# A tenth weight tile in a stage buffer, the last tile contracted mode by mode, the first output pair moved in halves

## The chip, the cores and the metric

The kernel runs on one core of a Trainium2 chip. The time is that of the whole program on the device, in microseconds (us); the number that is compared is the median over several executions. A profile is one further execution, recorded by the hardware profiler. The engines are TensorE (PE; its weight loads are listed as PEld), VectorE (DVE), ScalarE (ACT), GpSimd (POOL) and SyncE (SP). Loads are issued from the queues of GpSimd and SP and are carried out by 16 DMA engines.

## The reference

Two steps follow each other. The first is causal attention with a decay:

```
scores = scale * q @ k^T + (cum[i] - cum[j])      # cum: running sum of log f, causal
x      = softmax(scores) @ v                      # (8 batches, 8 heads, 576, 64)
```

The heads are then laid side by side, so x is (8, 576, 512). The second step mixes in frequency:

```
X = rfft(x) along the 576 positions; the lowest 64 modes are kept
Y[b, m, :] = X[b, m, :] @ (w_r[m] + i w_i[m])     # 64 modes, each with two 512 x 512 matrices
y = irfft(Y)
u = x + y
out = u + relu(u @ w_ch)
```

The weights w_r and w_i are 64 x 512 x 512 float32 each, 134 MB together. The output is (8, 576, 512) float32, 9.4 MB.

## The kernel before, in words

**Weights.** The weights are cut into NT = 64 tiles of 1 MB in bf16 (2 MB as float32; the load casts). Tile n < 32 holds a quarter of the input channels for MG = 4 modes; a tile from 32 on holds half of the input channels for M2 = 2 modes. They go through a ring of NRING = 9 buffers (`wpool`, tag `wb`). `emit_w_load(n)` issues two loads per tile, one for w_r and one for w_i, both on GpSimd's queue in program order (`pool_dma`, L89). The last tile, 63, has four loads: each mode's w_r and w_i apart. A load waits until TensorE has read the tile that was in its buffer nine tiles before, and until the load eight places ahead of it on the queue has landed. `next_w` (L645) issues the next tile, and is called after each tile's contraction.

**Attention.** It runs over 32 steps `s`, each one head of two batches; two steps form a pair `pr` of heads. The k, q and v of a pair are loaded into one of STG = 3 stage buffers (`QKVst`, L202), pair `pr` into buffer `pr % 3`. Between the pieces of a step, from step 9 on, the kernel contracts weight tiles (`emit_modes`, L119): for each mode and each of four output blocks a few 16-column matmuls with the weights as the stationary operand, summed in a PSUM tile `A`, then added by VectorE to `Yacc` (tiles below 32) or to the transposed spectrum `YTe`/`YT2` (tiles from 32 on, L164).

**After attention.** The loop at L814 contracts tiles 32 to 62. Between the tiles it computes `XW` = x @ w_ch (`emit_xw`, L746), the rows y of the modes that are already complete (`emit_y`, `emit_mid`), and adds these modes' share of the inverse transform to x and XW (`emit_part`, L788). `emit_xw` keeps its transposed x in `yy`'s memory.

**The tail.** Only the last 16 modes (`YT2[:, 1]`) are then open. The output is made in 20 jobs (L926): for each pair of batches four jobs of 256 rows (two blocks in two PSUM banks) and one of 128 rows that holds the last 64 of both batches. A job sums u (= x + y) and z (= u @ w_ch) in two PSUM tiles of two banks each. Each row block has an x part (L884: an identity matmul of what is already known) and a y part (L885: the inverse basis times the last modes' rows). Then ScalarE copies u out (`emit_u`, L896), VectorE takes max(z, 0) + u (`emit_o`, L909), and SP stores the result (L919). `y_rows` (L718) makes the rows of four batches: four transposes into `ply` and four matmuls with w_ch into `plw`. Evacuating them needs the rows in other partitions than they come in: job 0's rows go straight to their slot in `yy` (L846, L847), the others into `yl` (L851, L852) and from there by small DMAs on GpSimd's queue (L855). `emit_late(0)` serves batches 0 to 3, `emit_late(1)` batches 4 to 7; the second follows job 0's turn of the loop at L944. That turn writes job 1's u, and turn n in general writes job n's z interleaved with job n+1's u. All PSUM tiles of the tail come from one pool of two buffers for each of the tags u and z (eight banks, L832); the tiles `A`, `ply` and `plw` take turns with the jobs' tiles in it.

Job 0's x part is also used to keep TensorE busy around the last tile: `fill(times)` (L932) repeats it, eight 64x64 matmuls of 512 columns each time, in two groups of four that run side by side. Before the change it is called four times before the last tile, once after it, and once after the row products.

Of the kernel before, what the change touches and what calls it, by code (L numbers as in the profile page):

```python
# [21 lines left out]
def kernel(  # L22
# [11 lines left out]
    nc = tc.nc  # L34
# [56 lines left out]

    def emit_w_load(n):
        dc, g = tile_of(n)
        if n < NTH:
            wb = wpool.tile([128, MG, 2 * D], BF16, tag="wb", name="wb")
# [7 lines left out]
        else:  # L103
            wb = wpool.tile([128, 2, M2, 2 * D], BF16, tag="wb", name="wb")
# [14 lines left out]
    def emit_modes(n):  # L119
# [3 lines left out]
        if late["psM"] is None:  # L123
            z = late["psZ"].tile([128, 2, D], F32, tag="u", name="A")
            A = z[:, 0, 0 : NDC * nm * 2 * B].rearrange(
                "p (e m c) -> p e m c", e=NDC, m=nm
            )
        else:
            A = late["psM"].tile([128, NDC, nm, 2 * B], F32, tag="A", name="A")
        if n < NTH:  # L130
            terms = [
                (lambda mi, es, r=r: wb[:, mi, r * D + es : r * D + es + 128],
                 lambda m, r=r: XT3s[dc][:, r, :, m])
                for r in (0, 1)
            ]
        else:
            terms = [
                (lambda mi, es, t=t, r=r: wb[:, t, mi, r * D + es : r * D + es + 128],
                 lambda m, c0=c0, r=r: XT3s[2 + r][:, m, c0 : c0 + 2 * B])
                for t, c0 in ((0, B), (1, 0))  # L140
                for r in (0, 1)
            ]
        for mi in range(nm):
# [15 lines left out]
        else:  # L159
            n8 = nm * 2  # L160
            w = HM if g >= GL else HM // 2
            yt = late["YTe"] if g >= GL else late["YTs"][2 * g // GL]
            c0 = g * n8 % w
            nc.vector.tensor_tensor(  # L164
                _strided(
                    yt[:, 0, 0, c0 : c0 + 1], [[B * w, NDC], [w, B], [1, n8]]
                ),
                _strided(A[:, 0, 0, 0:1], [[nm * 2 * B, NDC], [1, B], [B, n8]]),
                _strided(
                    Yacc[:, 0, g * nm, 0:1], [[NM * 2 * B, NDC], [1, B], [B, n8]]  # L170
                ),
                ALU.add,
            )

    with ExitStack() as actx:
# [26 lines left out]
        QKVst = [  # L202
            {
                nm: stq.tile(
                    [128, 2, NR, Dh], F32 if nm == "v" else BF16, name=f"st{nm}{i}"
                )
                for nm in "kqv"
            }
            for i in range(STG)
        ]  # L210
# [441 lines left out]
        for s in range(NS + 1):  # L652
# [5 lines left out]
            if s < 10 and nload < min(NRING, 3 + 3 * s // 4):  # L658
                next_w()
            if s == 9:  # L660
# [27 lines left out]
    with ExitStack() as bctx:  # L688
# [12 lines left out]
        yy = bsb.tile([128, 2, B // 2, 2, D], BF16, name="yy")  # L701
        yls = [bsb.tile([128, 2, D], BF16, name=f"yl{i}") for i in range(2)]

        def row_slot(q, j, t, i):
            p0 = HM * ((j + t) % 2) + H2 * i
            return yy[p0 : p0 + H2, 1, 2 * q + j // 2, t, :]

        yflat = yy[:, :, :, :, :].rearrange("p l b t e -> p (l b t e)")
        xTs = [
            yflat[:, i * NDC * SP : (i + 1) * NDC * SP].rearrange(  # L710
                "p (e s) -> p e s", e=NDC
            )
            for i in range(3)
        ]
# [23 lines left out]
        with ExitStack() as cctx:  # L738
# [75 lines left out]
            while nmode < NT - 1:  # L814
                emit_modes(nmode)
                nmode += 1
                next_w()
# [11 lines left out]
            for a, sb in parts[done:]:  # L829
                emit_part(a, sb)  # L830

        psZ = bctx.enter_context(  # L832
            tc.tile_pool(
                name="psZ", bufs=2, space=bass.MemoryType.PSUM, reuse_waits="tile"
            )
        )
        late["psM"], late["psZ"] = None, psZ


        def emit_late(q):  # L840
            ply = psZ.tile([128, 2, D], F32, tag="z", name="ply")
            plw = psZ.tile([128, 2, D], F32, tag="u", name="plw")[:, 0, :]
            ply = ply[:, 0, 0 : D // 2].bitcast(BF16)
            y_rows(YT2[:, 1], 4 * q, ply, plw)
            if q == 0:
                nc.vector.tensor_copy(row_slot(0, 0, 0, 1), ply[0:H2, :])  # L846
                nc.scalar.copy(row_slot(0, 0, 1, 1), plw[0:H2, :])  # L847
            return ply, plw

        def emit_moves(q, pl):  # L850
            nc.vector.tensor_copy(yls[q][:, 0, :], pl[0])  # L851
            (nc.scalar.copy if q else nc.vector.tensor_copy)(yls[q][:, 1, :], pl[1])  # L852
            for j in range(1 - q, 4):
                for t in range(2):
                    nc.gpsimd.dma_start(  # L855
                        row_slot(q, j, t, 1), yls[q][H2 * j : H2 * j + H2, t, :]
                    )

        def pieces(job):
            b, sb, nb, _ = job  # L860
# [11 lines left out]
        def start(job):  # L872
            return tuple(
                psZ.tile([128, 2, D], F32, tag=tag, name="p" + tag) for tag in "uz"
            )

        def terms(job, ps, t, what):
            b, _, nb, _ = job
# [17 lines left out]
        def emit_u(job, ps):  # L896
            uo = wpool.tile([128, 2, 2, D], F32, tag="wb", name="uo")
            nc.scalar.copy(uo[:, 0, 0 : job[2], :], ps[0][:, 0 : job[2], :])  # L898
            return uo

        def emit_o(job, ps, uo, last):
            b, sb, nb, ty = job
            pz = ps[1][:, 0:nb, :]
            u_sb, o_sb = uo[:, 0, 0:nb, :], uo[:, 1, 0:nb, :]
            if ty == "Q":
                nc.scalar.activation(o_sb, pz, ACT.Relu)
                nc.gpsimd.tensor_tensor(o_sb, o_sb, u_sb, ALU.add)
            else:
                nc.vector.scalar_tensor_tensor(  # L909
                    o_sb, pz, 0.0, u_sb, ALU.max, ALU.add  # L910
                )
            if sb == 4:
                for h in range(2):
                    eng = nc.scalar if last and h else nc.sync
                    eng.dma_start(
                        out[b + h, 512:576, :], uo[64 * h : 64 * h + 64, 1, 0, :]
                    )
            else:
                nc.sync.dma_start(  # L919
                    out[b, 128 * sb : 128 * sb + 256, :].rearrange(  # L920
                        "(p r) e -> p r e", r=2
                    ),
                    o_sb,
                )
# [5 lines left out]
        jobs = [(*j, ty) for j, ty in zip(jobs, "NNNNNNNNNNNNNNNNNNNN")]  # L930
        ps = start(jobs[0])
        def fill(times):  # L932
            for _ in range(times):
                run(terms(jobs[0], ps, 0, "x"), terms(jobs[0], ps, 1, "x"), pin=True)

        fill(4)
        emit_modes(nmode)
        fill(1)
        pl = emit_late(0)
        fill(1)  # L940
        run(terms(jobs[0], ps, 0, "y"), terms(jobs[0], ps, 1, "y"))
        uo = emit_u(jobs[0], ps)
        emit_moves(0, pl)
        for n, job in enumerate(jobs):  # L944
            last = n == len(jobs) - 1
            zs = terms(job, ps, 1, "xy") if n else []
            us = []
            if not last:
                nxt = start(jobs[n + 1])
                us = terms(jobs[n + 1], nxt, 0, "xy")  # L950
            if job[1] == 4:
                run(us)
                run(zs)
            else:
                run(zs, us)
            if not last:
                uo_n = emit_u(jobs[n + 1], nxt)
            emit_o(job, ps, uo, last)
            if not last:
                ps, uo = nxt, uo_n  # L960
            if n == 0:
                emit_moves(1, emit_late(1))
# [28 lines left out]
```

## Time and profile before

| | us |
|---|---|
| median of 4 runs (438.86 to 441.13) | 440.1 |
| the profiled execution | 440.77 |
| its span, first to last instruction | 438.7 |
| PE busy | 361.7 (82%) |
| PEld busy | 247.2 (56%) |
| DVE busy | 263.6 (60%) |
| ACT busy | 225.0 (51%) |
| POOL busy | 129.0 (29%) |
| last tile's contraction starts | 401.33 |
| first store issued | 407.45 |

Mean granted TensorE clock: 0.851. The DMA engines moved 97.33 MB by the queues' own count, which takes weights as bf16; HBM was read for 163.73 MB. Weights arrive by 65 loads of w_r and 65 of w_i (63 of 512 KB and two of 256 KB each), with a median of 16.4 and 17.9 us from issue to landing.

The page divides the span into 40 slices. A digit is the busy share of a slice in tenths; PEclk is the granted TensorE clock in the same way. In a timeline, a line has the start, the duration, the engine, the source line, the operation, what it writes and reads, and in brackets the idle time ahead of it with what ended it.

### The profile page before, as it was taken

How to read it: one execution, taken by the hardware profiler on the slowest of the kernel's cores; microseconds unless marked ns; L12 is line 12 of the kernel's file. 1: busy time of each engine (PE TensorE's matmuls, PEld its weight loads, DVE VectorE, ACT ScalarE, POOL GpSimd, SP SyncE). 2: the span in 40 equal slices, each digit the busy share in tenths (PEclk: the TensorE clock that was granted, in tenths of full speed). 3: DMA queues.
4: the chain of work that ended last, by engine and by line, in shares of the span. 5: the costliest groups of instructions: out<-in, count | busy, mean ns of one | idle time of the engine just before them, and what ended most of it. 6: DMA issues, size and time to landing. Idle time of an engine off the chain costs nothing.

```text
span 438.7 us, 12229 instructions
## 1 busy us (share of the span) xinstructions
PE 361.7 (82%) x5276; PEld 247.2 (56%) x5293; DVE 263.6 (60%) x656; ACT 225.0 (51%) x339; POOL 129.0 (29%) x202
## 2 busy tenths in 40 slices
PE   2687799999887976877878886999989788879984
PEld 1454666776665665655656665666655444444442
DVE  5687778878565665665557677333234444653684
ACT  3688368876544437436456373233425333632663
POOL 7333332153233223232332221432232222200500
PEclk9997589999877758758668598799999896998997
DMA  8999999999999999999999999999999999992797
GB/s 181 235 235 244 231 235 239 232 195 238 233 216 235 227 221 236 212 237 233 214 237 211 211 212 210 211 211 212 211 211 211 212 211 211 211 203 43 248 368 290
DMA packets 50037, 97.33 MB, mean 222 GB/s; under 512 B 3488, under 2 KB 12192, under 8 KB 49984
## 3 DMA queue, kind: packets, MB, share of 16 engines
q0 software_dynamic: 46688, 86.39, 100.6%
q1 hardware_dynamic: 3216, 10.04, 6.2%
q8 instruction: 41, 0.67, 0.6%
q10 hardware_dynamic: 80, 0.13, 0.1%
q14 instruction: 12, 0.10, 0.1%
HBM read 163.73 MB, written 9.44 MB: 395 GB/s over the span
## 4 chain that ended last, share of the span: by engine, by line
PE 33%; DMA 29%; DVE 10%; ACT 10%; issue 5%; POOL 1%; DVEq 0%; ACTq 0%
DMA wb<-in_moe_w_i_dram 26%; ACT E L517 7%; PE pav L555 7%; PE ps L510 6%; PE A L147 5%; PE tp L458 5%; DMA stv<-in_v_dram 3%; PE pz L734 2%; DVE QTs L473 2%; PE px L598 2%; DVE uo L909 2%; PE vp L482 2%; ACT KT L471 2%; PE pu L734 2%; DVE XT L612 1%
## 5 line engine op out<-in xcount | busy, mean ns | idle before, releaser
L517 ACT ACTIVATE E<-ps 128x1024 bf16<-128x1024 f32 (+1 forms) x128 | 101.6, 854 | 23.8 <-PE ps L510 14.2
L147 PE MATMUL A<-XT,wb 128*128 128x16 bf16 x2048 | 72.8, 181 | 15.7 <-DMA wb<-in_moe_w_i_dram 10.9
L147 PEld LDWEIGHTS <-wb 128*128 128x128 bf16 x2048 | 65.9, 100 | 30.6 <-issue 13.0
L90 POOL DMA_DIRECT2D wb<-in_moe_w_r_dram x65 | 43.3, 666 | 128.7 <-DMA wb<-in_moe_w_r_dram 22.0
L510 PE MATMUL ps<-QTs,KT 64*128 64x64 bf16 (+4 forms) x384 | 55.4, 313 | 18.3 <-ACT E L517 17.1
L90 POOL DMA_DIRECT2D wb<-in_moe_w_i_dram x65 | 43.2, 664 | 82.2 <-DMA wb<-in_moe_w_i_dram 43.2
L555 PE MATMUL pav<-va,E 128*128 128x65 bf16 (+1 forms) x1088 | 53.3, 206 | 4.0 <-DVE x_all L577 3.5
L555 PEld LDWEIGHTS <-E 128*128 128x128 bf16 (+1 forms) x1088 | 43.7, 111 | 19.8 <-issue 9.6
L532 DVE TENSOR_TENSOR E<-E,trimask 128x256 bf16<-128x256 bf16 (+2 forms) x128 | 37.2, 303 | 19.9 <-ACT E L517 19.6
L770 ACT CAST XW<-pxw 128x512 bf16<-128x512 f32 x36 | 20.7, 587 | 37.5 <-PE pxw L763 25.2
L475 ACT COPY VT<-tp 128x640 bf16<-128x640 bf16 (+1 forms) x32 | 23.1, 756 | 32.4 <-PE tp L458 32.3
L806 ACT CAST XW<-pB 128x512 bf16<-128x512 f32 x36 | 20.9, 586 | 32.2 <-PE pB L734 27.0
L510 PEld LDWEIGHTS <-KT 64*128 64x128 bf16 x384 | 18.9, 97 | 30.3 <-issue 21.0
L805 DVE CAST x_all<-pA 128x512 bf16<-128x512 f32 x36 | 24.9, 692 | 17.0 <-PE pA L734 15.1
L763 PE MATMUL pxw<-wch,yy 128*128 128x512 bf16 x133 | 33.9, 387 | 1.0 <-issue 0.3
L471 ACT COPY KT<-tp 128x640 bf16<-128x640 bf16 (+1 forms) x32 | 22.1, 752 | 22.3 <-PE tp L458 22.3
L473 DVE COPY QTs<-tp 128x640 bf16<-128x640 bf16 (+1 forms) x32 | 23.3, 768 | 14.2 <-PE tp L458 14.1
L577 DVE TENSOR_TENSOR x_all<-pav,rcp 128x384 bf16<-128x384 f32 x64 | 29.1, 454 | 0.8
L734 PEld LDWEIGHTS <-ident_bf 64*64 64x64 bf16 (+1 forms) x328 | 16.5, 111 | 19.2 <-issue 11.8
L909 DVE SCALAR_TENSOR_TENSOR uo<-pz,uo 128x1024 f32<-128x1024 f32 (+1 forms) x20 | 21.9, 1116 | 6.7 <-ACT uo L898 2.6
L164 DVE TENSOR_TENSOR YTe<-A,Yacc 128x128 bf16<-128x128 f32 x16 | 5.9, 367 | 32.5 <-PE A L147 32.5
L566 DVE RECIPROCAL rcp<-pav 128x6 f32<-128x6 f32 x64 | 12.1, 189 | 21.2 <-PE pav L555 20.4
(128 smaller groups left out, 639.6 us busy)
## 6 DMA issues: line engine op xcount, KB each, us to landing
wb<-in_moe_w_r_dram POOLq DMA_DIRECT2D x63, 512.0 KB, 16.4
wb<-in_moe_w_i_dram POOLq DMA_DIRECT2D x63, 512.0 KB, 17.9
stv<-in_v_dram POOLq DMA_DIRECT2D x15, 576.0 KB, 15.1
out_dram<-uo SPq DMA_DIRECT2D x16, 512.0 KB, 3.8
stk<-in_k_dram POOLq DMA_DIRECT2D x16, 288.0 KB, 15.1
stq<-in_q_dram POOLq DMA_DIRECT2D x16, 288.0 KB, 15.1
out_dram<-uo SPq DMA_DIRECT2D x7, 128.0 KB, 3.4
stv<-in_v_dram SPq DMA_DIRECT2D x1, 576.0 KB, 5.5
```

The source lines that it names most:

```text
L90: tc.keep_in_program_order(nc.gpsimd.dma_start(dst, src))
L147: nc.tensor.matmul(A[:, eb, mi, :], lhsT=w_of(mi, eb * 128), rhs=x_of(m), start=(i == 0), stop=(i == len(terms) - 1),)
L471: nc.scalar.copy(rows(KTs[pr % 2][:, :, 0:S]), tv)
L473: nc.vector.tensor_copy(rows(QT[pr][:, :, :]), tv)
L510: nc.tensor.matmul(ps[:, b, o : o + n], lhsT=KTs[pr % 2][bs, h, jb * 128 : (jb + 1) * 128], rhs=QT[pr][bs, h, jb * 128 + c0 : jb * 128 + c ...
L517: nc.scalar.activation(E[:, :, piece * 512 : piece * 512 + w], ps[:, :, 0:w], ACT.Exp, scale=scale,)
L532: nc.vector.tensor_tensor(dg, dg, tr, ALU.mult)
L555: nc.tensor.matmul(pav[64 * half : 64 * half + w, slot, :], lhsT=E[:, b, c : c + (w - 1) * st + 1 : st], rhs=va[:, jb, b, :], start=(n == ...
L577: nc.vector.tensor_tensor(xo, pi, ri, ALU.mult)
L734: return nc.tensor.matmul(p, lhsT=lhsT, rhs=rhs, start=first, stop=not first, skip_group_check=True)
L763: nc.tensor.matmul(pxw[:, :], lhsT=xT[:, eb, i * 128 : (i + 1) * 128], rhs=wch[:, eb, :], start=(eb == 0), stop=(eb == NDC - 1),)
L909: nc.vector.scalar_tensor_tensor(o_sb, pz, 0.0, u_sb, ALU.max, ALU.add)
```

## The change

Three things are changed, and with them the way PSUM is divided in the tail.

1. The second stage buffer (buffer 1 of 3) is taken from a tile `wx` of its own in a pool on the other side of SBUF. The last pair that it serves is pair 13, which is read in steps 24 and 25. At step 28 (`s == 2 * (NPR - 2)`) one weight tile more is loaded, into `wx`; it is tile 34. From then on each tile is issued one contraction earlier. After tile 34 itself no tile is issued. Once tile 35 has been contracted, `open_late` closes `wx` and opens `yy` and `yls`, which were opened at the start of the phase before.
2. Tile 63 is contracted mode by mode and, within a mode, w_r before w_i, so that each group of eight matmuls needs one of the four loads. VectorE adds each mode by itself (`add_y`). The fillings are spread: one before the tile, one after mode 0, two between the w_r and w_i of mode 1, and half a one (u alone) after it: 36 matmuls instead of 48. The first matmul of mode 1 waits for VectorE's addition of mode 0.
3. Job 0's u is copied in two halves, and its result taken and stored in two halves. `ply` and `plw` have PSUM tiles of their own (`psL`), and job 1's u tile (`psU`) is free from the start; its z tile (`psX`) takes `psL`'s banks once `ply` and `plw` are read. ScalarE copies `ply` and VectorE does the two copies of `plw`. Job 1's u is written ahead of job 0's z rows, and job 1's z ahead of job 2's u. The rows of batches 4 to 7 are made after the sums of turn 3, in the second banks of job 4's two tiles, which that job does not use; they are copied by ScalarE after turn 3 and by VectorE after job 4's result, and their eight moves are issued then.

```diff
+    def wb_tile(n, *dims):
+        if n != late.get("nx"):
+            return wpool.tile([128, *dims], BF16, tag="wb", name="wb")
...
+        return late["wx"][:, 0 : math.prod(dims)].rearrange(
...
+        if n == NT - 1:
+            for mi in range(nm):
+                m = g * nm + mi
+                for hf, half in enumerate((terms[:2], terms[2:])):
+                    for w_of, x_of in half:
+                        for eb in range(NDC):
+                            tc.keep_in_program_order(
+                                nc.tensor.matmul(
+                                    A[:, eb, mi, :],
+                                    lhsT=w_of(mi, eb * 128),
+                                    rhs=x_of(m),
+                                    start=(eb == 0 and w_of is terms[0][0]),
...
+                    fill(mi, hf)
+                add_y(mi, mi + 1)
+            return
...
+            if s == 2 * (NPR - 2):
+                late["nx"] = nload
+                next_w()
...
                 emit_modes(nmode)
+                if nmode != late["nx"]:
+                    next_w()
                 nmode += 1
-                next_w()
+                if nmode == NTH + GL // 4:
+                    open_late()
...
-        def emit_u(job, ps):
+        def emit_u(job, ps, split=False):
             uo = wpool.tile([128, 2, 2, D], F32, tag="wb", name="uo")
-            nc.scalar.copy(uo[:, 0, 0 : job[2], :], ps[0][:, 0 : job[2], :])
+            for i in range(2 if split else 1):
+                bs = slice(i, i + 1) if split else slice(0, job[2])
+                nc.scalar.copy(uo[:, 0, bs, :], ps[0][:, bs, :])
...
-        fill(4)
-        emit_modes(nmode)
-        fill(1)
-        pl = emit_late(0)
-        fill(1)
-        run(terms(jobs[0], ps, 0, "y"), terms(jobs[0], ps, 1, "y"))
-        uo = emit_u(jobs[0], ps)
-        emit_moves(0, pl)
+        def fill(mi, hf):
+            for _ in range((1, 0, 1, 2, 0)[2 * mi + hf + 1]):
+                run(*(terms(jobs[0], ps, t, "x") for t in range(2)), pin=True)
+            if mi + hf == 2:
+                run(terms(jobs[0], ps, 0, "x"), pin=True)
+
+        fill(0, -1)
+        emit_modes(nmode, fill)
+        ply = psL.tile([128, D], BF16, tag="A", name="ply")
+        plw = psL.tile([128, D], F32, tag="plw", name="plw")
+        y_rows(YT2[:, 1], 0, ply[:, :], plw[:, :])
+        nc.vector.tensor_copy(row_slot(0, 0, 0, 1), ply[0:H2, :])
+        nc.scalar.copy(yls[0][:, 0, :], ply[:, :])
+        emit_moves(0, 0, (1,))
+        run(terms(jobs[0], ps, 0, "y"))
+        nc.vector.tensor_copy(row_slot(0, 0, 1, 1), plw[0:H2, :])
+        nc.vector.tensor_copy(yls[0][:, 1, :], plw[:, :])
+        emit_moves(1, 0, (1,))
...
+        lctx.close()
+        psPair[1]["z"] = psum(bctx, "psX")
+        uo = emit_u(jobs[0], ps, True)
         for n, job in enumerate(jobs):
...
-            if job[1] == 4:
+            if n == 0:
+                run(us)
+                run(zs)
+            elif n == 1:
+                run(zs)
+                run(us)
+            elif job[1] == 4:
                 run(us)
                 run(zs)
             else:
                 run(zs, us)
+            if n == 3:
+                y_rows(
+                    YT2[:, 1], 4, nxt[1][:, 1, 0 : D // 2].bitcast(BF16), nxt[0][:, 1, :]
+                )
             if not last:
                 uo_n = emit_u(jobs[n + 1], nxt)
-            emit_o(job, ps, uo, last)
+            emit_o(job, ps, uo, n == 0, last)
+            if n == 3:
+                nc.scalar.copy(yls[1][:, 1, :], nxt[0][:, 1, :])
+            if n == 4:
+                nc.vector.tensor_copy(
+                    yls[1][:, 0, :], ps[1][:, 1, 0 : D // 2].bitcast(BF16)
+                )
...
-            if n == 0:
-                emit_moves(1, emit_late(1))
```

## The prediction

> **What bounds the kernel now.** I read the time slices of the page first, then busy time by stretch, the GpSimd queue's own timeline, and last VectorE's timeline and the chain of waits at the end. The slices:
>
> ```profile
> DMA  8999999999999999999999999999999999992797
> GB/s 181 235 235 244 231 235 239 232 195 238 233 216 235 227 221 236 212 237 233 214 237 211 211 212 210 211 211 212 211 211 211 212 211 211 211 203 43 248 368 290
> ```
>
> The 16 DMA engines are busy without a gap for 35 of 40 slices, at a flat 211 GB/s once only weights move. Those are bytes as bf16; the fp32 side is twice that, 422 GB/s. So the program is 400 us of loads and then a tail of 38 us, in which slice 37 (395 to 406 us) moves almost nothing. By stretch (the last three numbers are the granted clock, the DMA share and GB/s):
>
> ```profile
> 265.00:275.00 10.00, 6.29 (x142) 5.29 (x139) 7.24 (x19) 1.85 (x4) 1.82 (x3) 0.76 1.12 211
> ...
> 393.00:396.00 3.00, 1.76 (x42) 1.13 (x38) 1.12 (x2) 1.12 (x2) 0.00 (x0) 1.00 0.77 144
> 396.00:400.00 4.00, 4.00 (x31) 1.54 (x32) 1.75 (x3) 1.17 (x2) 0.00 (x0) 0.57 0.43 79
> 400.00:401.00 1.00, 1.00 (x24) 0.50 (x20) 0.00 (x0) 0.00 (x0) 0.00 (x0) 1.00 0.06 16
> ```
>
> The engines do not finish together: the share sinks from 393 on and the last bytes come at 400. The last four loads, issued at 378.22, 380.43, 382.98 and 385.45, take 18.1, 17.1, 15.9 and 14.7 us, so they land at 396.3, 397.5, 398.9 and 400.15. TensorE is then at half clock. GpSimd's queue at the end of attention, where the new buffer acts:
>
> ```profile
> 259.97 0.72 POOL L90 DMA_DIRECT2D wb<-in_moe_w_i_dram  x1
> 265.93 0.71 POOL L90 DMA_DIRECT2D wb<-in_moe_w_r_dram  x1 [5.24 <-PE A L147]
> 266.64 0.72 POOL L90 DMA_DIRECT2D wb<-in_moe_w_i_dram  x1
> 274.62 0.71 POOL L90 DMA_DIRECT2D wb<-in_moe_w_r_dram  x1 [7.25 <-PE A L147]
> ```
>
> GpSimd waits 5.24 and 7.25 us for TensorE to free a ring slot. Yet the DMA share in that stretch is 1.12, the same as everywhere. VectorE in the tail:
>
> ```profile
> 404.68 0.69 DVE L852 CAST yl<-plw 128x512 bf16<-128x512 f32 x1 [0.60 <-ACT yy L847]
> 406.20 1.23 DVE L909 SCALAR_TENSOR_TENSOR uo<-pz,uo 128x1024 f32<-128x1024 f32 x1 [0.83 <-ACT uo L898]
> 407.34 0.42 DVE L851 COPY yl<-ply 128x512 bf16<-128x512 bf16 x1
> 409.39 2.43 DVE L909 SCALAR_TENSOR_TENSOR uo<-pz,uo 128x1024 f32<-128x1024 f32 x2 [1.64 <-issue]
> 412.22 1.82 DVE L909 SCALAR_TENSOR_TENSOR uo<-pz,uo 128x1024 f32<-128x1024 f32 x2 [0.40 <-PE pz L734]
> 414.64 1.22 DVE L909 SCALAR_TENSOR_TENSOR uo<-pz,uo 128x1024 f32<-128x1024 f32 x1 [0.60 <-ACT uo L898]
> ```
>
> From 416.16 on the same pattern returns every 6.76 us (416.16, 422.92, 429.68). The chain there alternates TensorE's z sums with VectorE's results and has no spare engine in it, so a shift of job 6's result reaches the end whole.
>
> **What the Trainium skill says.** "DMA: Bandwidth & Descriptors", Specifications, gives 435 GB/s as the fabric's ceiling for a core. The trace agrees: 422 is 97% of it, so earlier issue cannot raise the rate. The same page, "Why a DMA increments its semaphore by 16 and not by 1": a load counts as landed only when all 16 engines have posted. The share sinking for 7 us ahead of the landing at 400.15 fits. "TensorE: Matmul & The Clock Gate", Part 1: the clock is halved or restored by activity over a free-running window of about 3.4 us. The trace has half clock from about 396.4 to 399.9. "PSUM — Partial Sum Buffer", Terms: two engines may not be on one bank and quadrant at once. This fits the wait that the change adds between the two modes, which share a bank; the trace before has no such wait.
>
> **The extra weight tile: nothing.** Tile 34 goes to the stage buffer at step 28 without waiting for a slot, so each later tile is issued one slot earlier, and the waits of 5.24 and 7.25 us should shrink or go. The bytes and the 130 weight loads are the same, in the same queue order. When GpSimd issued again at 274.62, how far was the DMA from idling? At 279.88 it waits for the landing of the load of 259.97; loads take about 2.45 us each (0.5 MB at 211 GB/s), so those of 265.93 and 266.64 land near 282.3 and 284.8. There were 10 us in hand. The cover is this backlog; without it, the loss would be at most the excess of a wait over it. Value taken 0; between 0 and -1 if in other executions the quick DMA engines run dry. The new waits of GpSimd on VectorE (stage buffer read by step 25) are past by then. The pool opened late (yy, yls) waits only for tile 34's matmuls, six tiles ahead of its first use.
>
> **The last tile, mode by mode: +0.25.** Before, TensorE ran 32 filling matmuls (8 steps of four, 0.42 us a step at half clock and 0.21 at full) from 399.09 to 401.22, and only then the tile from 401.33 to 402.28. So TensorE, not the landing at 400.15, was late. Afterwards the same 32 filling matmuls stand in between: 0.85 at half clock to 399.94, mode 0 (16 matmuls of 0.03, and 0.1 for the switch, 401.22 to 401.33 above) to 400.53, two steps to 400.96, 8 matmuls to 401.30, four steps to 402.16, the last 8 to 402.50. Then VectorE adds half a tile: 0.37 less 64 x 1.06 ns (0.681 against 1.224 us for 512 and 1024 elements) is 0.30, from 402.55 to 402.85. Filling of two steps runs beside it to 402.93, and the transposes follow 0.1 later, near 403.0 against 402.77. The new wait (mode 1 behind VectorE's add of mode 0) holds all of TensorE's queue, but two filling steps and the switch, 0.53, cover its 0.35. Without that cover it would cost about 0.3. With all waits on DMA instead of filling, the gain would be 24 matmuls, 0.7; with the clock still low, the loss 0.5. I keep -0.7 to +0.5.
>
> **First job and the rows.** Call the first transpose P (402.77 before). Before, in us after P: job 0's result 3.43 to 4.66, job 1 at 6.62, job 2 at 7.85, job 3 at 9.45, job 5 at 11.87, job 6's z sum starts at 11.59 and its result at 13.39. Job 1's u had waited for the evacuation of the second u bank (start 405.42, just after the cast of 404.68 ended), and its z stood behind the second row product (8 matmuls from 406.40 to 407.5) and interleaved with job 2's u.
> Afterwards: rows ready at 0.44 (transposes) and 1.29 (product). VectorE copies 0.44 to 0.85, casts twice 0.69 (a cast's time goes by free size) to 2.67; ScalarE copies to about 1.1 (128x512, 0.59 to 0.74). TensorE, no longer waiting for a bank: job 0's u rows to 1.53, job 1's u (4 steps) to 2.4, job 0's z rows to 2.83, job 1's z to 3.7, job 2's u to 4.56. ScalarE: two halves of 0.586 to 2.74 (0.16 more than one of 1.014), then job 1 to 3.75. VectorE: halves of 0.62 (0.681 and 1.224 bound them) from 2.86 to 4.1, job 1 to 5.33. Job 2 waits for ScalarE (4.76 to 5.77): result 5.8 to 7.03. Job 3's z stands beside job 4's u, whose bank ScalarE frees at 5.77: result near 7.4. So job 1 leads by 2.5, jobs 2 and 3 by 2.05.
> GpSimd's moves: the one for jobs 2 and 3's u is issued at 1.15 and lands 1.7 later, needed at 3.95; the one for their z at 2.77, landing at 4.5, needed at 4.8. Four more follow at 0.5 each, needed from 8.5. SP has one more store to issue, 24 instead of 23; stores land in 2.7 to 4.5 us and nobody waits for their slots within nine jobs.
>
> **The second rows: the lead mostly goes back.** Before, the product for the second half of the batches sat in VectorE's bubble of 1.64. Now it comes after job 3's sums. TensorE: from 7.13, 1.2 for the product to 8.35 (406.40 to 407.60), job 5's u to 9.2, job 4's z to 9.65; so job 4's result ends at 10.5 and the cast of its bank's other half, 0.42, at 10.95. Only then is the bank free, and job 6's z starts at 11.0, against 11.59: 0.59 earlier. The eight moves for this half are issued from 11.05 instead of 5.3, and job 10 needs the first at 15.6. They took 1.7 to 4.9 us before, so at worst 0.4 late.
>
> **The sum.** 0 + 0.25 - 0.59 = -0.35. The profiled execution took 440.77 (span 438.7 and 2.07 around it), so 440.4; that execution is 0.67 above the median, so against 440.1 it is 439.7. With the bounds of its terms and the spread of the runs (438.86 to 441.13), 438.9 to 440.6.
>
> **Rivals.** (1) The lead of 2.05 survives, because the product of the second rows finds TensorE idle. For it: TensorE idles 0.3 to 0.5 at several places in each period. Against: 1.2 + 0.42 stand in one chain in front of job 6's bank. 438.05 on the median. (2) The extra tile does work: the landing comes up to 2 us sooner because the quick engines no longer run dry and less is left to the slow ones. For it the two waits, against it the share of 1.12. About 438. (3) Slower: the clock. Twelve filling matmuls fewer (36 instead of 48) and more waits among the first jobs; if one more window of 3.4 us falls to half clock there, 1.75 us of TensorE work is lost. It decides from a fifth of a window on (0.35 of 1.75). One window gives 441.5, two 443.2. Against it: 1.00 was granted from 400 to 434 although TensorE was busy 85% of 409 to 434. (4) The change does not do what it says: the tile in the stage buffer lands no sooner. That is part of the forecast.
>
> **How the numbers follow.** Forecast 0.53, rival 1 0.25, rival 2 0.08, rival 3 0.14. The range 438.0 to 441.3 holds almost all of the first, about half of rivals 1 and 2 and a third of rival 3, some 0.8. A change of 0.5%, 2.2 us, is about what a measurement of this kernel can tell from none: bounds 437.9 and 442.3. Below the lower one falls half of rival 1, half of rival 2 and 0.03 of the forecast, 0.20; above the upper one about 0.6 of rival 3 and 0.01 of the forecast, 0.10; between them 0.70.
>
> **What would show it.** Right: GpSimd's waits on TensorE between 255 and 278 gone and DMA share still 1.12; last landing near 400; transposes at about 403.0; job 1's result some 4.2 after them; job 4's result late by TensorE and job 6's z started by the cast of its bank. Wrong: a landing before 399, a half clock in the tail, a wait for moved rows at job 10, or job 4 following job 3 without a gap.

## The result, and the profile after

The changed kernel takes 442.68 us (median of 38 runs, 439.64 to 445.7) against 439.4 us for the kernel before (59 runs, 437.88 to 443.13). The ratio is 1.0065, with a 95% interval of 1.005 to 1.008: by this ratio 2.9 us slower, where 439.7 (438.0 to 441.3) was predicted. The runs of the changed kernel also lie further apart, over 6.1 us instead of 5.3, and 16 of the 38 are above 443. The profiled execution took 441.33 (span 439.3). It is one of the quicker ones, and the one of before was one of the slower, so the two spans differ by only 0.6. Three executions of the experiments below lay far above the others of their kernel (663.18 of again, the one that was profiled, 556.48 of filled_wait and 445.05 of product_later); they are in the medians of the table, but not in its ratios nor in the counts of executions.

The slices of the changed kernel, DMA share and GB/s:

```profile
DMA  8999999999999999999999999999999999991798
GB/s 180 235 235 243 232 236 238 235 218 230 236 212 237 233 215 237 208 237 236 211 237 211 211 211 211 211 211 211 212 211 210 212 211 211 211 191 36 242 363 295
```

The load phase is as it was: 211 GB/s without a gap. GpSimd's queue at the end of attention:

```profile
267.27 0.71 POOL L90 DMA_DIRECT2D wb<-in_moe_w_r_dram  x1 [2.59 <-PE A L185]
...
276.32 0.71 POOL L90 DMA_DIRECT2D wb<-in_moe_w_r_dram  x1 [6.49 <-PE A L185]
...
283.65 0.72 POOL L90 DMA_DIRECT2D wb<-in_moe_w_r_dram  x1 [3.87 <-PE A L185]
```

The waits on TensorE did not go. Before, the three long ones were 3.51, 5.24 and 7.25 us (at 259, 266 and 275); now they are 2.59, 6.49 and 3.87, each some 9 us later, 13.0 in all instead of 16.0. The last four loads are issued at 377.40 to 385.58 (before: 378.22 to 385.45). So nothing was lost there and little could be won. Now VectorE's timeline in the tail of the changed kernel (start, duration, instruction, and in brackets the idle time ahead of it):

```profile
402.96 0.41 DVE L989 COPY yy<-ply 32x512 bf16<-32x512 bf16 x1 [0.65 <-PE ply L772]
...
405.36 2.42 DVE L953 SCALAR_TENSOR_TENSOR uo<-pz,uo 128x512 f32<-128x512 f32 x3
409.80 2.50 DVE L953 SCALAR_TENSOR_TENSOR uo<-pz,uo 128x1024 f32<-128x1024 f32 x2 [2.02 <-issue]
413.83 0.69 DVE L953 SCALAR_TENSOR_TENSOR uo<-pz,uo 128x512 f32<-128x512 f32 x1 [1.53 <-PE pz L785]
414.44 0.41 DVE L1030 COPY yl<-pz 128x512 bf16<-128x512 bf16 x1
414.84 1.22 DVE L953 SCALAR_TENSOR_TENSOR uo<-pz,uo 128x1024 f32<-128x1024 f32 x1
416.70 2.43 DVE L953 SCALAR_TENSOR_TENSOR uo<-pz,uo 128x1024 f32<-128x1024 f32 x2 [0.63 <-PE pz L785]
```

P, the first transpose of the last rows, is 402.53 here and was 402.77. Job 0's two halves and job 1 follow from 405.36, that is P + 2.83, as predicted (2.86). Then comes a gap of 2.02 that was not predicted: job 2's result starts at P + 7.27 instead of P + 5.8. From there the lead is gone, and job 6's result starts at P + 14.17, where it was P + 13.39 before. What holds job 2 stands in TensorE's timeline:

```profile
407.04 0.38 PE L785 MATMUL pu<-XW,ident_bf 64*64 64x512 bf16 x1
408.87 0.40 PE L785 MATMUL pz<-yy,BIl 64*64 64x512 bf16 x2 [1.45 <-DMA yy<-yl]
...
411.08 0.38 PE L772 MATMUL pz<-ident_bf,YT 128*128 128x128 bf16 x4
...
414.91 0.40 PE L785 MATMUL pz<-x_all,ident_bf 64*64 64x512 bf16 x1 [0.31 <-DVE yl L1030]
```

TensorE stands still for 1.45 us until a move of rows (`yy<-yl`) has landed. The second product (411.08) overwrites a half of job 2's z banks, so it waits for job 2's result (409.80 to 411.03). Behind the product come the sums of job 4, its result (413.83) and the cast that VectorE makes next (414.44); job 6's z sums (414.91) wait for that cast. The whole wait is handed down to the end.

Why is that move late? The queues at that time, GpSimd's and ScalarE's, and the stores on SP's:

```profile
404.60 2.98 POOL L900 DMA_DIRECT2D yy<-yl  x6 [18.49 <-ACT yl L990]
413.72 3.91 POOL L900 DMA_DIRECT2D yy<-yl  x8 [6.14 <-ACT yl L1028]
```

```profile
403.41 0.59 ACT L990 COPY yl<-ply 128x512 bf16<-128x512 bf16 x1 [4.67 <-DVE yy L989]
```

```profile
406.08 2.06 SPq L965 DMA_DIRECT2D out_dram<-uo  x3
```

In the source the move that job 2's z needs (product rows of batch 1) is the second of the six. In the built program it is the fourth. This is GpSimd's instruction order with the semaphores (counters) that each waits for, and the matmul of job 2's z that waits for the move. Activation and DVE are the counters of ScalarE and VectorE; a DMASW counter is raised when a move lands:

```
191 L900 DMACopy yy<-yl_5118 32x512 [waits DMASW2_49,Activation_49,Pool_49]
192 L900 DMACopy yy<-yl_5118 32x512 [waits DMASW3_49]
193 L900 DMACopy yy<-yl_5118 32x512 [waits DMASW4_49]
194 L900 DMACopy yy<-yl_5118 32x512 [waits DMASW5_49,DVE_49]
...
10029 L785 Matmult pz<-yy,BIl 64x512 [waits DMASW5_49]
```

The first three are the transposed rows (they need ScalarE's copy only); the product rows, which need VectorE's cast, come after them. The six are issued 0.5 us apart, the fourth at 406.11. From issue to landing the six took 1.7, 1.7, 1.7, 2.7, 3.1 and 2.8 us: the fourth is the first that meets job 0's stores, issued from 406.08 on. 406.1 plus 2.7 is the 408.8 at which TensorE goes on. (ScalarE's copy, 403.41, also began 0.44 later than predicted: it waited for VectorE's copy out of the same `ply`.)

The program of the kernel before has the same order of the six, with this move fourth. There it was issued at P + 3.50, no store was issued before 407.45 (P + 4.68), the move landed after 1.7 us, and job 2's z sums read the rows only at about P + 6.0. The change asks for them at P + 4.9 and, by halving job 0's result, sends the first store off at P + 3.55.

### The profile page after: what moved, and what is told of

Its sections match the earlier page's. It is cut to its first block, busy times and chain, and to the rows that moved or that the text cites. A ratio compares the mean times of both kernels' runs of the same rounds, so it can differ in the third digit from the quotient of the medians.

```text
span 439.3 us, 12210 instructions
## 1 busy us (share of the span) xinstructions
PE 359.4 (82%) x5263; PEld 246.4 (56%) x5281; DVE 263.9 (60%) x658; ACT 225.2 (51%) x340; POOL 128.9 (29%) x202
## 4 chain that ended last, share of the span: by engine, by line
PE 31%; DMA 30%; ACT 12%; DVE 10%; issue 5%; POOL 1%; DVEq 0%; ACTq 0%
DMA wb<-in_moe_w_i_dram 26%; ACT E L558 8%; PE pav L596 6%; PE ps L551 5%; PE A L185 5%; PE tp L499 5%; DMA stv<-in_v_dram 3%; PE px L639 2%; DVE QTs L514 2%; ACT KT L512 2%; PE pz L785 2%; PE vp L523 2%; DVE uo L953 1%; DVE XT L653 1%; PE pu L785 1%
## 5 line engine op out<-in xcount | busy, mean ns | idle before, releaser
L185 PE MATMUL A<-XT,wb 128*128 128x16 bf16 x1984 | 70.4, 181 | 15.9 <-DMA wb<-in_moe_w_i_dram 11.1
L185 PEld LDWEIGHTS <-wb 128*128 128x128 bf16 x1984 | 63.5, 99 | 30.2 <-DMA wb<-in_moe_w_i_dram 12.2
L90 POOL DMA_DIRECT2D wb<-in_moe_w_r_dram x64 | 42.4, 663 | 126.7 <-PE A L185 24.2
L90 POOL DMA_DIRECT2D wb<-in_moe_w_i_dram x64 | 42.2, 660 | 81.2 <-DMA wb<-in_moe_w_i_dram 40.4
```

The costliest lines, as they stand in the source:

```text
L90: tc.keep_in_program_order(nc.gpsimd.dma_start(dst, src))
L185: nc.tensor.matmul(A[:, eb, mi, :], lhsT=w_of(mi, eb * 128), rhs=x_of(m), start=(i == 0), stop=(i == len(terms) - 1),)
```

## The experiments

The kernels ran in three groups (four rows of the table each), every group beside its own runs of the kernel before, whose median was 439.65, 439.55 and 439.51. P is read from each kernel's own profile.

| kernel | median | ratio to before (95%) |
|---|---|---|
| again | 442.29 | 1.0066 (1.0039 to 1.0092) |
| moves_in_order | 439.49 | 0.9999 (0.9979 to 1.0018) |
| no_extra_tile | 442.6 | 1.0063 (1.0034 to 1.0092) |
| extra_tile_alone | 438.82 | 0.9989 (0.9972 to 1.0007) |
| changed_again | 441.9 | 1.006 (1.004 to 1.0079) |
| filled_wait | 441.61 | 1.0042 (1.0023 to 1.0061) |
| moved_third | 440.4 | 1.0016 (0.9997 to 1.0035) |
| product_later | 439.49 | 0.9999 (0.9983 to 1.0015) |
| first_moves_in_order | 439.55 | 1.0 (0.9986 to 1.0014) |
| second_moves_in_order | 442.96 | 1.0093 (1.0062 to 1.0124) |
| filled_four | 441.55 | 1.0047 (1.0029 to 1.0066) |
| fewer_fillers | 438.08 | 0.9981 (0.9966 to 0.9996) |

### Late moves, or the load phase?

**again** is the changed kernel, without an edit.

> The changed kernel once more, for a second profile of it beside the ones below. Theory M (late moves): the move of the product's rows for batch 1 stands fourth in GpSimd's queue, so TensorE's z sums of job 2 wait over 1 us for it (1.45 us in the first profile), and job 6 comes late with it. Theory L (load phase): the extra tile lets the last weights land later in some executions (400.5 to 403 instead of 399.9). Both expect 442.7 median; M expects the wait in this profile again, 1 to 4 us, and the last contraction at the same 398.8 to 399.5; L expects the last landing to have moved, and the tail behind it not.

It gave times only. 442.29 repeats the result.

**moves_in_order** pins each move behind what is already on GpSimd's queue:

```diff
     def emit_moves(t, q, js):
         for j in js:
-            nc.gpsimd.dma_start(
+            tc.keep_in_program_order(nc.gpsimd.dma_start(
                 row_slot(q, j, t, 1), yls[q][H2 * j : H2 * j + H2, t, :]
-            )
+            ))
```

> The changed kernel with the 14 moves of rows issued in the order of the source, so that the product's rows for batch 1 go second and not fourth. M: the move is issued at P + 2.7 instead of P + 3.6 (P is the first transpose of the last rows), its rows land 1.0 to 1.5 us sooner, job 2's z sums no longer wait, and the whole is 1 to 1.5 us faster than the changed kernel: about 441.3. L: nothing changes, 442.7.

439.49: the whole loss is gone, twice what the wait of 1.45 explains. The order on the other engines is the same to the instruction. VectorE's and GpSimd's timelines of this kernel, where P is 402.80:

```profile
408.55 2.58 DVE L953 SCALAR_TENSOR_TENSOR uo<-pz,uo 128x1024 f32<-128x1024 f32 x2 [0.50 <-ACT uo L946]
412.58 0.69 DVE L953 SCALAR_TENSOR_TENSOR uo<-pz,uo 128x512 f32<-128x512 f32 x1 [1.45 <-PE pz L785]
413.19 0.41 DVE L1030 COPY yl<-pz 128x512 bf16<-128x512 bf16 x1
413.62 1.23 DVE L953 SCALAR_TENSOR_TENSOR uo<-pz,uo 128x1024 f32<-128x1024 f32 x1
415.46 2.43 DVE L953 SCALAR_TENSOR_TENSOR uo<-pz,uo 128x1024 f32<-128x1024 f32 x2 [0.62 <-PE pz L785]
```

```profile
404.87 0.52 POOL L900 DMA_DIRECT2D yy<-yl  x1 [19.71 <-ACT yl L990]
405.80 2.45 POOL L900 DMA_DIRECT2D yy<-yl  x5 [0.41 <-DVE yl L994]
```

The move is issued at 405.80 and lands 1.7 us later, at 407.5; TensorE's first matmul that needs it runs at 407.51. Job 2's result is at P + 5.75 and job 6's at P + 12.66, 1.5 us sooner after P than in the changed kernel's profile and 0.7 sooner than before. That the median is still only as good as before has to do with what lies ahead of P (see the last tile, below).

**no_extra_tile** leaves the tail as changed and takes the extra load of part 1 out; all weight tiles come from the ring of nine again, and `yy` and `yls` are opened at the start of the phase (the second stage buffer stays in its own pool):

```diff
-        if n != late.get("nx"):
+        if True:
             return wpool.tile([128, *dims], BF16, tag="wb", name="wb")
...
-            if s == 2 * (NPR - 2):
-                late["nx"] = nload
-                next_w()
...
+        wxctx.close()
+        open_late()
...
-                if nmode != late["nx"]:
-                    next_w()
+                next_w()
                 nmode += 1
-                if nmode == NTH + GL // 4:
-                    open_late()
```

> The changed kernel without its first part: no weight tile in the stage buffer, everything after the loads as in the changed kernel. M: as the changed kernel, 442.7 within 0.7. L: as before or below it, 439 to 440.5.

442.6: the loss stays, so it is not the extra tile's.

**extra_tile_alone** is the kernel before with part 1 alone (`wb_tile`, `stage`, `open_late` and the load at step 28):

> The kernel before with the first part of the change alone (one more weight tile in the stage buffer from step 28 on). M: no difference to before, within 0.7 us. L: slower than before by most of the whole change, 1.5 to 3.3 us.

438.82, between 1.2 less and 0.3 more than before by its interval. The load phase as a cause falls. What part 1 is worth is not settled further.

### Where the other half comes from

no_extra_tile's profiled execution took 444.66, near the top of what the changed kernel shows. It has the same wait, and this is what follows it (in a stretch: its length, busy time and number of instructions of PE, PEld, DVE, ACT and POOL, then the granted clock, the DMA share and GB/s):

```profile
404.00:408.00 4.00, 3.58 (x37) 1.69 (x37) 3.77 (x5) 2.74 (x5) 2.97 (x6) 1.00 0.30 93
408.00:412.00 4.00, 2.84 (x23) 1.48 (x23) 1.26 (x2) 1.52 (x2) 0.00 (x0) 0.71 0.61 219
412.00:416.00 4.00, 3.78 (x19) 1.39 (x20) 1.23 (x1) 1.05 (x2) 0.00 (x0) 0.50 0.65 254
416.00:420.00 4.00, 3.69 (x44) 1.87 (x42) 2.24 (x3) 2.04 (x3) 3.42 (x7) 0.93 0.35 84
```

TensorE runs at half clock from 409.7 to 416.5. The profile of the changed kernel has 1.00 in all four of these stretches. So the next question was whether the gap brings the half clock on.

**changed_again** is the changed kernel once more, without an edit.

> The changed kernel on the chip of the three below. Theory W (wait alone): the wait of 1.45 us at job 2's z sums costs 1.45 us in every execution; the spread comes from elsewhere. Theory H (wait, then half clock): TensorE is idle for more than half of 407.4 to 410, the clock's window that holds this gap halves the next one or two windows in most executions, and these cost up to 4 us more. H expects the profile to show about 0.5 granted somewhere between 408 and 418 if this execution is above 442, and 1.00 throughout if it is below 441.5; W expects no such split.

Its profiled execution took 440.69, below 441.5, and the clock was 1.00 from 393 to 430, with the same wait (1.49) and job 6 at P + 14.22. That fits H, but so would chance, as no profile of this very kernel above 442 was had. Of the 71 executions of it in the result and the two repetitions, 29 are above 443.

**second_moves_in_order** has the first six moves in the changed kernel's order, written out and pinned, and pins the eight of the second half as well:

```diff
-        emit_moves(1, 0, (1,))
-        for j in (2, 3):
-            for t in range(2):
-                emit_moves(t, 0, (j,))
+        emit_moves(0, 0, (2, 3))
+        emit_moves(1, 0, (1, 2, 3))
```

> The reverse: the first six moves as the changed kernel has them, the eight of the second half in the order of the source. M: as the changed kernel, 441.9 to 442.5. Q: about 440.5 to 441.

**first_moves_in_order** pins only where `q == 0`, that is the first six.

> Only the first six moves in the order of the source; the eight of the second half as the changed kernel has them (the four of the product first, so that what job 10's u sums need is fifth). Theory M: what counts is the first group alone: 439.5. Theory Q (second group): the fifth move lands too late for job 10 in many executions, and holds the part of the loss above the wait at job 2: about 441.

442.96 (six executions) and 439.55: the order of the first group carries the loss, that of the second makes no difference that could be measured. Q falls. second_moves_in_order's profile (execution of 442.73, P = 402.08) has TensorE's wait, and a half clock behind it:

```profile
408.42 0.64 PE L785 MATMUL pz<-yy,BIl 64*64 64x512 bf16 x2 [1.45 <-DMA yy<-yl]
```

```profile
404.90:408.30 3.40, 2.07 (x20) 1.02 (x21) 2.42 (x3) 2.03 (x3) 2.22 (x5) 1.00 0.61 192
408.30:411.70 3.40, 3.28 (x23) 1.70 (x23) 1.23 (x1) 1.01 (x1) 0.00 (x0) 0.51 0.46 175
```

These are two stretches of 3.40 us, the window length that the Trainium skill states ("TensorE: Matmul & The Clock Gate", Part 1, which says that the window is free-running). In the first, TensorE was busy for 2.07 of 3.40; the next ran at 0.51, each 64x64 matmul of 512 columns taking 0.64 instead of 0.40. Job 6's result is at P + 15.66: 1.5 us for this one window. In no_extra_tile, P is 402.78 and job 6's result at 420.10, that is P + 17.3: 3.1 us for two.

Why did the changed kernel and changed_again, with the same gap, keep full clock in their profiles? In the thirteen traces read here the clock changes only at steps of 3.413 us (half-clock stretches last 3.41, 6.83, 10.24 us and so on). With windows counted in such steps from each trace's own changes of the clock, the four profiles with an unfilled gap are these:

| profile | windows that hold the gap, and TensorE's busy time in each | clock of the window that follows each |
|---|---|---|
| second_moves_in_order | 404.95 to 408.36: 2.02 | 0.50 |
| no_extra_tile | 406.29 to 409.70: 1.92 | 0.50 |
| the changed kernel | 404.67 to 408.08: 2.66; 408.08 to 411.50: 2.48 | 1.00; 1.00 |
| changed_again | 404.01 to 407.42: 2.63; 407.42 to 410.84: 2.48 | 1.00; 1.00 |

Where the gap falls into one window, half clock follows; where two windows share it, it doesn't. So one and the same gap can cost 1.5 us in one execution and 3 to 4.6 in another. This is a reading of four traces; no run shifts the gap on purpose.

**filled_wait** repeats job 2's own first matmuls in the gap, 16 more in all:

```diff
+            if n == 2:
+                for _ in range(4):
+                    run(terms(job, ps, 1, "x"), pin=True)
```

> The changed kernel with 16 more matmuls in front of job 2's z sums (its first matmuls four times more, each time from the start, so the sums are the same). They take about 1.7 us where TensorE waited 1.45, so the rows come as late as before, but TensorE isn't idle. W: as the changed kernel or 0.3 slower, 442.5 to 443, the same spread. H: no half clock behind it; 440.5 to 441.3, the highest of the runs below 443.

**filled_four** does it with job 3's u beside them, 32 more:

```diff
+            if n == 2:
+                for _ in range(4):
+                    run(
+                        terms(job, ps, 1, "x"),
+                        terms(jobs[3], nxt, 0, "x"),
+                        pin=True,
+                    )
```

> The wait at job 2 filled as in the kernel with the filled wait, but with 32 matmuls in place of 16: job 2's z and job 3's u sums together, so that four quadrants of the array are busy at once instead of two, as in TensorE's usual stretches. Same lateness of the rows, sums the same. Theory H (half clock behind the gap): if the clock goes by how much of the array is busy, 440.3 to 441.2 and no run above 443; W (wait alone, no clock): 441.6 to 442.5, as the other filling.

Neither came out as expected in its median: 441.61 and 441.55, under the changed kernel's medians by 0.3 to 1.1. The top did go: 1 of 21 and 0 of 10 executions are above 443, where the changed kernel has 29 of 71. In both profiles the clock is full past the gap and job 6 still late (P + 14.20 and P + 14.18), since the rows land as late. In filled_four's:

```profile
404.00:408.00 4.00, 3.91 (x58) 2.66 (x55) 3.32 (x5) 3.00 (x4) 2.98 (x6) 1.00 0.41 123
408.00:412.00 4.00, 3.84 (x48) 2.36 (x43) 2.45 (x2) 1.01 (x1) 0.00 (x0) 1.00 0.64 237
```

Its execution took 442.44 all the same: from the start of VectorE's last two results at 432.76 to the end of the span are 7.6 us, where the profiles of the changed kernel have 6.2. The last stores take their own time, between 6.1 and 7.6 in the profiles here. So W falls (executions without the gap lack the slow top, and two profiles show the half clock), and H holds for the top. By their ratios the filled kernels are 1.8 (1.0 to 2.7) and 2.1 (1.3 to 2.9) above before; the 1.5 of late rows lies within both, and what is left above it, which in one profile is the last stores, can't be told from noise.

**moved_third** gives a smaller dose of lateness, with the order on TensorE, VectorE and ScalarE unchanged:

```diff
-        emit_moves(1, 0, (1,))
-        for j in (2, 3):
-            for t in range(2):
-                emit_moves(t, 0, (j,))
+        emit_moves(0, 0, (2,))
+        emit_moves(1, 0, (1,))
+        emit_moves(0, 0, (3,))
+        emit_moves(1, 0, (2, 3))
```

(on top of moves_in_order)

> The moves as in the kernel with the moves in order, but the product's rows for batch 1 third instead of second: issued 0.5 us later, TensorE's, VectorE's and ScalarE's instructions in the same order. Both: rows 0.5 to 1.5 us later than in second place, a wait of 0 to 1.2 us. W: 439.5 plus that wait, 439.5 to 440.7. H: the same as W as long as the gap is below 1 us, up to 442 if it isn't.

440.4: between the second place (439.49) and the fourth (442.3), but by its interval (0.9997 to 1.0035) not to be told from the kernel before. The dose came out smaller than meant. In second place the move waits for VectorE's cast and is issued at P + 3.00; in third place GpSimd is done with the move ahead of it soon after the cast, and issues it at P + 3.08, not 0.5 us later. It landed after 1.7 us, TensorE did not wait, and job 6's result is at P + 12.66, like moves_in_order. So this run says little about a half dose.

### Two tries at something better

**product_later** makes the second product behind job 4's z sums, in that job's own banks, with the moves in order:

```diff
-            if n == 3:
+            if n == 4:
                 y_rows(
-                    YT2[:, 1], 4, nxt[1][:, 1, 0 : D // 2].bitcast(BF16), nxt[0][:, 1, :]
+                    YT2[:, 1], 4, ps[1][:, 1, 0 : D // 2].bitcast(BF16), ps[0][:, 1, :]
                 )
```

> The kernel with the moves in order, and the second product of rows behind job 4's z sums instead of behind job 3's (in the free half of job 4's own banks), to see whether the place of this product is worth something. If its 8 matmuls (1.2 us) stand on the path to job 4's and 5's results, these come 0.7 to 1.2 us sooner, but the cast that frees job 4's bank comes 0.4 to 1 us later, and job 6's z sums with it: 439.5 to 440.5. If job 6 is bound by job 5's result instead: 438.5 to 439.2.

439.49, no difference: job 4's result comes 1.2 us sooner, job 5's later.

**fewer_fillers** adds to product_later that the repeated matmuls between the last two groups of the last tile are left out:

```diff
-            for _ in range((1, 0, 1, 2, 0)[2 * mi + hf + 1]):
+            for _ in range((1, 0, 1, 0, 0)[2 * mi + hf + 1]):
                 run(*(terms(jobs[0], ps, t, "x") for t in range(2)), pin=True)
-            if mi + hf == 2:
-                run(terms(jobs[0], ps, 0, "x"), pin=True)
```

> A version that might beat both: all moves in order, the second product behind job 4's z sums, and the fillers between the last tile's first and second weights of mode 1 taken out (20 matmuls, 1.06 us at full clock by the profile of the changed kernel: 400.63 to 401.69). If the last weights have landed by then (last traffic near 399.9), the rows come 0.9 to 1.1 us sooner, and the end with them: 438.4 to 438.8. If TensorE then waits for the landing instead, or falls to half clock for want of filling: 439.3 to 440.5.

438.08, ratio 0.9981 (0.9966 to 0.9996): below both kernels, against before by 0.8 us by the ratio (0.2 to 1.5) and by 1.4 by the medians. TensorE's timeline of it:

```profile
398.35 0.56 PE L169 MATMUL A<-XT,wb 128*128 128x16 bf16 x16
399.39 0.56 PE L169 MATMUL A<-XT,wb 128*128 128x16 bf16 x16
400.27 0.40 PE L772 MATMUL ply<-ident_bf,YT 128*128 128x128 bf16 x4
```

Mode 1's 16 matmuls run in one piece, with no wait for a landing ahead of them, and the transposes come 1.92 us after the first of mode 0 (398.35). In the changed kernel these are 402.53 and 399.37, 3.16 apart, at full clock in both profiles. The last load landed at about 399.3 here and at 400.3 there, where the last group started only at 401.69: the fillers had stood in the way of weights that were already there.

## Why the prediction was wrong

**What bounds the kernel: right.** Until the last landing nothing changed, and the tail decides. That the load rate has no room rests on the flat 211 GB/s in both kernels; the 422 that was set beside the ceiling of 435 are bytes as they are read, and no run here shows on which side that ceiling acts.

**The extra tile, 0 (0 to -1): right in size, not quite in its picture.** extra_tile_alone gives -0.5 by its ratio (-1.2 to 0.3). The waits of GpSimd did not go; they shrank from 16.0 to 13.0 us in all and came some 9 us later.

**The last tile mode by mode, +0.25 (-0.7 to +0.5): too small.** Read off the clock, the transposes come as they did: 402.80 in moves_in_order and 402.77 before, both with half clock between 396 and 400. But in the former profile the last load had landed 0.8 us sooner. A fair count starts at an event that both have, the contraction of tile 62 once its last load has landed, and compares equal clocks:

| tile 62's contraction to the first transpose, us | full clock | half clock, from 395 to 396.5 on |
|---|---|---|
| last tile as before | 5.99 (extra_tile_alone, 395.01 to 401.00) | 7.62 (before, 395.15 to 402.77) |
| mode by mode | 7.25 (changed kernel, 395.28 to 402.53; four more profiles 7.25 or 7.26) | 8.47 to 8.85 (five profiles; moves_in_order 394.33 to 402.80) |
| mode by mode, 20 matmuls fewer | 6.01 (fewer_fillers, 394.26 to 400.27) | |

The step costs 1.26 at full clock and 0.85 to 1.23 at half (one profile each of the old form). The sum had taken the fillers to go through without a pause. Built, the second half of the first fillers waits for VectorE's copy of the part before them, and mode 0 starts some 0.9 us later than two filling steps would let it:

```profile
398.81 0.40 PE L785 MATMUL pz<-x_all,ident_bf 64*64 64x512 bf16 x1 [0.45 <-DVE x_all L856]
```

The fillers between the groups then reach past the last landing: the transposes come 2.25 us after it in the changed kernel, and 1.0 after it in extra_tile_alone and in fewer_fillers (which has the same wait).

**First job and rows: this is the step that failed, in one sentence.** "The one for their z at 2.77, landing at 4.5, needed at 4.8" took the moves in the order of the source. Built, it was the fourth on the queue: issued at P + 3.58, landing 2.7 us later at P + 6.3 with job 0's stores under way, and needed at P + 4.9. The margin of 0.3 us in that sentence could not carry a queue position that had not been looked up. Once the move has the place that the sentence gave it, the rest of the step holds: job 2's result at P + 5.75 (predicted 5.8). Even so there was luck in it: issued at P + 3.00 and landed 1.7 us later, the rows came just as TensorE read them (P + 4.71), with none of the margin left. The start of the first move, P + 1.15, was too early as well (P + 2.07): ScalarE's copy began 0.44 late, behind VectorE's copy out of `ply`, and the issue followed its end by 0.6 us. It cost nothing, as that move landed at P + 3.8 and TensorE read its rows at P + 3.86 without a wait.

**Second rows, -0.59: right with the moves in order.** Job 6's z sums start at P + 10.86 there (predicted 11.0), the cast ends at P + 10.80 (predicted 10.95), and job 6's result comes 0.73 sooner than before. In the changed kernel the sums start at P + 12.38. The worry about job 10's rows was not needed: their order makes no difference.

**The sum.** -0.35 was predicted. With the moves in order it is -0.16 by the medians (-0.9 to 0.8 by the ratio's interval). That this is near -0.35 is partly luck: the last tile took 0.6 to 1.0 more than its term, and the 0.73 of the second rows, and what the extra tile may have given, paid for it. The 2.8 us by which the changed kernel is above that are the term that the sum left out: 1.5 us of late rows in every profile with the late move and, in part of the executions, half clock behind the gap.

**The rivals.** Rival 3 had the right price (1.75 for a window; 1.5 measured) and half of the right cause: not the fewer fillers, since leaving out 20 more made the kernel faster and its profile has full clock through the tail, but a wait among the first jobs, which it named without a place or a length. Its chance was put at 0.14 because the clock before had been full at 85% busy; it was not asked what a gap of 1.5 us would do to a window. The signs listed as wrong named a wait for moved rows at job 10; the wait came at job 2.

## What to carry to other kernels

Where a scheduler orders a queue, read the place of each transfer in the built program before giving it a time, and pin the order of those that someone waits for first. A transfer whose slack is less than one issue slot of its queue has none: half a microsecond of queue and one of store traffic made a kernel that was as fast as the one before 2.9 us slower. A short gap on TensorE is to be priced twice, once as lateness and once as the half clock that may follow. And two profiles are to be compared from an event that they share, at equal clock: by its absolute times the last tile seems to cost nothing, from the contraction before it about 1 us.

## What the runs showed of the hardware

- A gap of 1.45 to 1.5 us was followed by half clock in two of four profiles that had an unfilled one. In windows of 3.41 us on the grid on which the clock changes, the one ahead of the half clock had TensorE busy for 2.02 (second_moves_in_order), 1.92 (no_extra_tile) and, before the change, 2.17 (393.09 to 396.50); the two profiles that kept full clock had 2.48 or more in every window of the gap. Busy time alone doesn't settle it: in filled_wait a window with 1.90 (390.60 to 394.02) was followed by full clock.
- In no_extra_tile the window at half clock (409.71 to 413.12) had TensorE busy all through, 3.41 of 3.41, and the next one was at half clock as well. Why the clock did not come back there stays open.
- A 32 KB move from SBUF to SBUF on GpSimd's queue landed 1.7 us after its issue while nothing else moved, and after 2.5 to 3.1 us once 256 to 512 KB output stores were being issued (the first six moves of the changed kernel and of moves_in_order; before the change, with the first store 1.3 us later after P, all six took 1.7 to 1.9).
